# Attention beside a spectral filter: block 0 of x worked on alone at first, its key weights loaded behind it, the last chunk normalised in halves, and the planner's weights

## The chip, the cores and the metric

The kernel runs on one core of a Trainium2 chip, as one program. The metric is the device time in microseconds of one execution. Times from several executions are given as a median; the profile is taken from one execution.

## What is computed

The reference, cut to what matters (x has 2048 rows of 448 numbers in bfloat16, 16 heads of 28):

```
g   = sigmoid(sum(x * gate_w, -1))
q, k, v = split(x @ wqkv)                      # 16 heads of 28
p   = softmax(q @ k.T / sqrt(28))              # 2048 x 2048 for each head
a   = (p @ v) @ wo
b   = irfft2(rfft2(x) * (w_r + i w_i))         # over rows and columns
out = g * a + (1 - g) * b
```

## The kernel before

**Packs, units, chunks.** The heads are worked on in four groups of four, and the queries in four blocks of 512, which gives 16 chunks (group, query block). A chunk meets 16 key tiles of 128 keys, each a pack of four units, one for each head of the group: scores of 128 keys by 512 queries. There are 256 packs, 1024 units. A pack is taken either by ACT or by DVE. For ACT, a "tile" of two units is written by PE into one of two double banks (psA and psB, called "row" work), and one ACTIVATE takes the exponential of both units into the ring P of 20 units, or, for the first five packs, into slots of VS (line 902). For DVE, PE writes one unit at a time into a bank psX (`d_run`), DVE turns the scores into bits of an approximate power of two (line 931), and three shifted copies follow (line 937). In both cases PE then multiplies the probabilities by the values and sums into psV ("column" work, `pv_run`): one pass for a pack of ACT, four for a pack of DVE.

**The rest is background.** Transposes of x, projections to keys, queries and values, the four steps of the Fourier filter (f1, f2 and f3, i1, i2) and the output products are "units" of the planner: one or more PE operations into a psX bank and the evacuations that follow.

**The planner sets the order.** `Plan` runs while the program is built. It keeps a time for each engine and fills in the next operation by score: the due time of a unit, its `rush`, weights from `CFG`, and `seg`, which overrides these weights in each sixteenth of the stream (segment 17 holds once no score is left to be made). Only the order on each engine comes out of it; on the chip every engine runs its own list in that order and waits by semaphores. `pe_step` (line 640) chooses for PE: a ready tile for ACT goes first, and otherwise the offer with the lowest score that fits before the next tile is due. Offers come from value passes, open units, new units, scores for DVE (weight `w_d`) and "zero" matmuls. These multiply by zeros into an open accumulation or a free bank. `load` (line 259) sums the columns that PE worked in the last 3.413 us; under `z_hard` a zero matmul gets the score -20 ahead of everything, and under `z_soft` it is offered where there is nothing else. `step` (line 312) chooses for the other engines; ACT takes an exponential when one is ready, unless an operation of negative priority is, and it takes an operation that belongs to DVE (`alt`) only before the keys are complete (`early`).

**The head.** `loads` (line 1110) issues the constants and then the weights of the first group (keys, then queries; 112 columns each) on ACT's queue, and the four blocks of x on SP's, followed by the value weights and the rest. `head` (line 1186) makes for each block b of 512 rows two units "xT" of eight transposes, which wait only for that block's DMA; each is evacuated by DVE or ACT. `first` (line 1229) projects the keys of group 0 for block b and the queries of block 0: four matmul passes, a square on ACT, a norm product of PE with `selk` or `selrow` into the same bank ("sel"), and an evacuation to KT or QT with scale. Between them, DVE copies the key weights into the padded form Wk and POOL the query weights into Wq (line 1152). When the minimum over all keys is known, "w" computes a weight for each key (`o_wt`, line 1225), by which the values are multiplied (`weigh`, line 1346). Until then no value pass and no pack of DVE can start.

**The tail.** A chunk is normalised by way of DMAs (`norms`), except the last: `norm_last` (line 1522) takes 128 queries at a time, four times, on DVE. It transposes psV into osb, takes the reciprocal of the sums, multiplies by the gate, multiplies the values, and transposes the product into ON[3]. `final` (line 1535) makes for each of the 16 output tiles of 128 rows four products ("pre") and then the product with the last group; for the last four tiles the latter waits for `norm_last`. DVE evacuates tiles 0 to 11, and ACT tiles 12 to 15; a DMA writes them.

## Time and profile before

| | |
|---|---|
| time, median of 3 runs | 403.59 us (402.97 to 403.9) |
| time of the profiled execution | 402.86 us |
| its span | 401.1 us |
| PE busy | 385.3 us (96%) |
| DVE busy | 345.8 us (86%) |
| ACT busy | 384.2 us (96%) |
| POOL busy | 127.2 us (32%) |
| granted TensorE clock, mean | 0.999 |

The span runs from the first instruction's start to the last end that the profile holds; the time of the execution also has what lies around it. A group of the profile is named by its line, its engine, its operation and out<-in; behind "x" stands the number of instructions, and behind the bar the busy time and the mean of one in ns. Many helpers share a line (953 is every matmul), so tiles tell groups apart. A row of the order of time begins with its start and its length in us; the square bracket holds the idle time before it and what ended it. A row of the busy time by stage holds the stage, its length, the busy time of PE, weight loads, DVE, ACT and POOL with their counts, the granted clock, the share of the DMA engines and GB/s.

### The profile page before, as it was taken

What the parts mean: (1) busy time and instruction counts of PE and PEld (TensorE: products, weight loads), DVE (VectorE), ACT (ScalarE), POOL (GpSimd) and SP (SyncE); (2) the same over time, 40 slices, a digit from 0 to 9 for tenths busy, and PEclk for the clock granted to TensorE, in tenths of its full rate; (3) what the DMA queues carried; (4) which work ended last, traced back from release to release, by engine and by line L of the source; (5) the groups of instructions that cost most, each with busy time, mean ns of one, the idle gap of its engine ahead of it and who ended that gap; (6) DMA issues with size and microseconds to landing.
All of it is one profiled execution on the core that took longest, in us unless ns stands there. A gap on an engine that the chain in (4) does not pass through costs nothing.

```text
span 401.1 us, 12723 instructions
## 1 busy us (share of the span) xinstructions
PE 385.3 (96%) x5246; PEld 133.7 (33%) x5246; DVE 345.8 (86%) x633; ACT 384.2 (96%) x423; POOL 127.2 (32%) x176
## 2 busy tenths in 40 slices
PE   7999999999999999999999999999999999999995
PEld 3534433233333322332233222333334322223333
DVE  3649999978888898987899878899998999899994
ACT  3799999999999999999999999999999999999992
POOL 0121504532232136344334644547047520001000
PEclk9999999999999999999999999999999999999999
DMA  8700012100201202120112112022010001010012
GB/s 250 177 30 6 4 17 42 29 29 3 69 4 41 65 3 66 38 64 11 37 55 83 43 35 58 12 69 80 2 29 2 30 1 31 25 46 31 25 52 70
DMA packets 24394, 17.69 MB, mean 44 GB/s; under 512 B 15731, under 2 KB 19744, under 8 KB 24336
## 3 DMA queue, kind: packets, MB, share of 16 engines
q1 hardware_dynamic: 23264, 16.59, 15.2%
q8 instruction: 41, 0.67, 0.7%
q10 hardware_dynamic: 1072, 0.29, 0.4%
q14 instruction: 17, 0.14, 0.1%
HBM read 14.71 MB, written 1.97 MB: 42 GB/s over the span
## 4 chain that ended last, share of the span: by engine, by line
ACT 57%; PE 26%; issue 10%; DVE 4%; DMA 1%; ACTq 0%; DVEq 0%
ACT P L902 55%; PE psX L953 9%; PE psV L953 7%; PE psB L953 5%; PE psA L953 4%; DVE VS L931 2%; DMA Qf<-in_A_wqkv_dram 1%; ACT VS L902 1%; DVE VS L937 1%; PE psX L1198 1%; ACT xT L1205 0%; DVE Vb L1330 0%; ACT sq L1552 0%; DVE ost L1552 0%; DVE QT L1244 0%
## 5 line engine op out<-in xcount | busy, mean ns | idle before, releaser
L902 ACT ACTIVATE P<-psB 128x1024 bf16<-128x1024 f32 x198 | 215.5, 1088 | 0.2
L902 ACT ACTIVATE P<-psA 128x1024 bf16<-128x1024 f32 x198 | 215.5, 1089 | 0.1
L931 DVE TENSOR_SCALAR VS<-psX 128x512 int16<-128x512 f32 x212 | 139.4, 682 | 20.2 <-PE psX L953 19.6
L937 DVE TENSOR_SCALAR VS<-VS 128x2048 int16<-128x2048 int16 x159 | 103.5, 699 | 0.5
L953 PEld LDWEIGHTS <-KT 32*128 32x128 bf16 (+1 forms) x1040 | 46.6, 91 | 145.7 <-issue 142.4
L953 PE MATMUL psB<-QT,KT 32*128 32x512 bf16 x406 | 79.2, 382 | 5.4 <-ACT P L902 4.7
L953 PE MATMUL psA<-QT,KT 32*128 32x512 bf16 x406 | 79.7, 383 | 1.7 <-ACT P L902 1.3
L953 PE MATMUL psV<-VS,Vb 128*32 128x512 bf16 x868 | 76.3, 385 | 0.4 <-DVE osb L1510 0.2
L953 PE MATMUL psV<-P,Vb 128*32 128x512 bf16 x792 | 73.6, 385 | 0.0
L953 PE MATMUL psX<-QT,KT 32*128 32x512 bf16 x212 | 71.0, 383 | 0.5 <-DVE VS L931 0.2
L953 PEld LDWEIGHTS <-Vb 128*32 128x32 bf16 x1660 | 33.5, 94 | 57.5 <-issue 53.6
L1439 POOL TENSOR_TENSOR t<-FX,Wf 128x452 bf16<-128x452 f32 x32 | 31.7, 1013 | 41.5 <-DVE FX L1436 20.5
L1519 POOL TENSOR_TENSOR xtok<-osb,RB 128x512 bf16<-128x512 f32 x12 | 15.3, 1275 | 73.9 <-DVE VS L937 48.3
L1183 POOL TENSOR_TENSOR sq<-QT 128x512 bf16<-128x512 bf16 x16 | 16.6, 1041 | 41.2 <-DVE QT L1264 18.1
L1493 POOL TENSOR_TENSOR UZ<-tab 128x225 bf16<-128x225 f32 (+1 forms) x32 | 17.8, 583 | 23.1 <-DVE VS L937 19.1
L1183 POOL TENSOR_TENSOR sq<-KT 128x512 bf16<-128x512 bf16 x12 | 12.5, 1042 | 31.6 <-DMA omg<-gd 13.9
L953 PE MATMUL psX<-xT,Wk 112*32 112x512 bf16 x256 | 20.1, 383 | 0.0
L953 PE MATMUL psX<-Wv,xT 112*32 112x113 bf16 (+1 forms) x512 | 19.5, 262 | 0.0
L953 PE MATMUL psX<-xT,Wq 112*32 112x512 bf16 x240 | 19.5, 384 | 0.0
L1447 POOL TENSOR_TENSOR t<-t,t 128x226 bf16<-128x226 bf16 x32 | 17.5, 570 | 5.2 <-DVE VS L937 4.5
L953 PE MATMUL psX<-Bd,UZ 112*32 112x452 bf16 x256 | 18.7, 358 | 0.0
L953 PEld LDWEIGHTS <-xT 112*32 112x32 bf16 (+1 forms) x576 | 11.0, 96 | 10.5 <-issue 8.2
(104 smaller groups left out, 305.1 us busy)
## 6 DMA issues: line engine op xcount, KB each, us to landing
tab<-c_tab SPq DMA_DIRECT2D x16, 256.0 KB
RB<-rgd SPq DMA_DIRECT2D x60, 64.0 KB
xtok<-in_A_x_dram SPq DMA_DIRECT2D x4, 448.0 KB
out_dram<-ost SPq DMA_DIRECT2D x6, 224.0 KB
rs<-osb SPq DMA_DIRECT2D x60, 2.0 KB
Wf<-in_B_w_r_dram SPq DMA_DIRECT2D x31, 28.1 KB
Wf<-in_B_w_i_dram SPq DMA_DIRECT2D x31, 28.1 KB
Qf<-in_A_wqkv_dram SPq DMA_DIRECT2D x2, 294.0 KB
```

The costliest lines, as they stand in the source:

```text
L902: k.nc.scalar.activation(out=out, in_=k.psS[e["grp"]][:, 0:n, :], func=ACT.Exp, scale=LN2_128)
L931: k.nc.vector.tensor_scalar(out=k.VS[:, slot, 512 * h:512 * h + 512], in0=bank, scalar1=float(BITS0), scalar2=BITS_MIN, op0=ALU.add, op1=A ...
L937: k.nc.vector.tensor_scalar(out=k.VS[:, dst, :], in0=k.VS[:, src, :], scalar1=float(SHIFTS[v - 1]), scalar2=None, op0=ALU.add)
L953: self.nc.tensor.matmul(out, lhsT=lhsT, rhs=rhs, start=start, stop=stop, skip_group_check=True, **kw)
L1183: (self.nc.vector if e == "DVE" else self.nc.gpsimd).tensor_tensor(out=sq[:, :], in0=src, in1=src, op=ALU.mult)
L1198: nc.tensor.transpose(out=bb[0:C, 512 * ci + 128 * k:512 * ci + 128 * k + 128], in_=self.xtok3[:, 4 * b + k, C * c:C * c + C], identity=se ...
L1439: ts.append(pl.op("POOL", 1.07, lambda e, i=i, q=q: nc.gpsimd.tensor_tensor(out=self.t12[i][q][:, :].rearrange("p (r f) -> p r f", r=2), i ...
L1447: (nc.vector if e == "DVE" else nc.gpsimd).tensor_tensor(out=t1[:, FP * q:FP * q + FP], in0=t1[:, FP * q:FP * q + FP], in1=t2[:, FP - FP * ...
L1493: nc.gpsimd.tensor_tensor(out=z, in0=a, in1=b, op=ALU.subtract if q else ALU.add)
L1519: prev = pl.op("POOL", 1.3, lambda e, G=G, j=j: nc.gpsimd.tensor_tensor(out=self.ON[G][:, 512 * j:512 * j + 512], in0=self.osb[:, :], in1= ...
```

## The change

**Loads.** SP issues block 0 of x, then the key weights of group 0, then blocks 1 to 3. ACT's queue keeps the constants and the query weights. The planner's landing times for these DMAs are lower.

**Head.** Block 0's transposes, its keys and its queries get the highest rush (8) and the earliest places. The queries of block 0 are made right behind its keys, ahead of block 1. The transposes of block 1's second half wait for the norm product of block 0's keys, and those of blocks 2 and 3 for that of block 0's queries. ACT may evacuate transposes only of blocks 0 and 1 (`x_act=4`).

**Choice of PE.** While the load is under `z_hard`, every column operation with an efficiency over 0.8 gets the bonus of 20, not the zero matmul alone; the zero matmul's score is 9 before the bonus.

**Choice of ACT.** ACT also takes evacuations that belong to DVE once no score and no exponential is left.

**Tail.** `norm_last` takes 256 queries at a time, twice. Tiles 0 to 11 of the output may be evacuated by ACT.

**Weights.** `z_hard` is 3450 by default (was 3250), and many weights of segments are different.

The diff, cut:

```diff
@@ step
-            if eng == "ACT" and o.alt is not None and not early and o.eng != "ACT":
+            if eng == "ACT" and o.alt is not None and not early and o.eng != "ACT" and (any(self.s_left) or self.next_exp < len(self.tiles)):
                 continue
@@ pe_step
+        w = self.load(t) if any(self.s_left) and t >= self.zero_from else 1e9
+        hard = w < c["z_hard"] and self.started
+
-        def offer(score, kind, n, go):
+        def offer(score, kind, n, go, eff=1.0):
             nonlocal best
             cost = self.pe_cost(kind, n)
+            if hard and kind != "row" and eff > 0.8:
+                score -= 20.0
...
-        if any(self.s_left) and t >= self.zero_from:
-            w = self.load(t)
-            if w < c["z_hard"] or (best is None and w < c["z_soft"]):
-                hard = w < c["z_hard"] and self.started
-                if self.v_open(t) and self.started:
-                    offer(-20.0 if hard else 9.0, "col", 512, lambda: self.zero(t, "col", None))
...
+        if w < c["z_hard"] or (best is None and w < c["z_soft"]):
+            if self.v_open(t) and not self.started:
+                offer(9.0, "full", 512, lambda: self.zero(t, "full", None))
+            elif self.v_open(t) or fb:
+                offer(9.0, "col", 512, lambda: self.zero(t, "col", None if self.v_open(t) else fb[0]))
@@ CFG
+    last=((0, 2), (2, 2)), x_act=4,
-    z_hard=3250
+    z_hard=3450
     seg={
-        0: dict(d_open=4, w_hungry=0, z_hard=3550),
-        1: dict(d_open=4, z_hard=3550),
-        2: dict(w_new=2.0, z_hard=3550),
-        3: dict(pv_min=3, hungry=2),
-        4: dict(hungry=4),
-        5: dict(v2_due=3.1, hungry=4),
-        6: dict(hungry=4, prio_shift=3),
-        7: dict(w_pv=0.6, z_hard=3450, tol=0, v2_at=0.5, prio_shift=3),
+        0: dict(d_open=4, w_hungry=0, z_hard=3550, w_open=1.2),
+        1: dict(tol=0),
+        3: dict(tol=0.15),
+        4: dict(ahead=2, tol=0.15),
+        5: dict(v2_due=3.1, hungry=4, w_pv=0.6, tol=0.15),
+        6: dict(hungry=4, prio_shift=3, tol=0.15),
+        7: dict(w_pv=0.6, tol=0, v2_at=0.5, prio_shift=3),
...
-        10: dict(z_hard=3550),
-        11: dict(z_hard=3550),
+        10: dict(z_hard=3550, d_open=4),
+        11: dict(z_hard=3550, g_at=[1.1, 4.3, 8.0]),
...
-        13: dict(ring_urg=8, w_pv=0.2, prio_shift=3.5, z_hard=3550, d_urg=1, w_new=2.0),
-        14: dict(w_open=0.2, prio_shift=3.5, ahead=1, w_late=2, w_pv=0.2, ring_urg=6, w_new=2.0),
-        15: dict(prio_shift=3.5, w_open=0.2, w_late=2, w_pv=0.2, z_hard=3350, w_d=1.7, w_new=2.0),
-        16: dict(w_d=1.7, w_new=2.0, ring_urg=6),
-        17: dict(w_new=2.0),
+        13: dict(ring_urg=4, w_pv=0.2, prio_shift=3, z_hard=3550, d_urg=1, w_new=2.0, z_soft=3800, w_late=2),
+        14: dict(w_open=0.2, prio_shift=3.5, ahead=1, w_late=2, w_pv=0.2, ring_urg=4, w_new=2.0, w_due=4, pv_min=2, z_soft=3800),
+        15: dict(prio_shift=3.5, w_open=0.2, w_late=1, w_pv=0.2, z_hard=3350, w_new=1.2, w_due=4, pv_min=2, z_soft=3800),
+        16: dict(sw_pen=1.5),
+        17: dict(z_soft=3800, w_new=1.2),
@@ loads
-        self.d_w0 = [self.dma(..., 4.0, eng="ACT", prio=0) for i, o in ((0, D), (1, 0))]
         for b in range(4):
-            self.d_x.append(self.dma(..., (4.4, 5.6, 6.9, 8.2)[b], **fast))
+            self.d_x.append(self.dma(..., (4.0, 4.8, 5.55, 6.3)[b], prio=0 if b == 0 else 5, **fast))
+            if b == 0:
+                self.d_w0 = [self.dma(..., 4.2, eng=e, prio=1, ...) for i, o, e in ((0, D, "SP"), (1, 0, "ACT"))]
@@ head
-                u = pl.unit(-0.2, "xT", due=-1, rush=6.0 if b == 0 else CFG["x_rush"])
+                u = pl.unit(-0.2 if b == 0 else -0.185 + 0.01 * b, "xT", due=-1, rush=8.0 if b == 0 else CFG["x_rush"])
...
-                u.mm(tr, n=128, count=8, eff=0.0, deps=[self.d_x[b], self.d_cst])
+                u.mm(tr, n=128, count=8, eff=0.0, deps=[self.d_x[b], self.d_cst, sel[0] if (b, cp) == (1, 1) else sel[1] if b > 1 else None])
...
-                self.o_xT[b].append(u.use("DVE", dict(DVE=0.62, ACT=0.95), ev, alt="ACT", prio=2))
+                self.o_xT[b].append(u.use("DVE", dict(DVE=0.62, ACT=0.95), ev, alt="ACT" if 2 * b + cp < CFG["x_act"] else None, prio=2))
+            k = self.k_ready[0][b] = self.first(0, b, "k0", self.selk, 0)
...
+            if b == 0:
                 self.q_ready[0] = self.first(1, 0, "q0", self.selrow, 2)
...
+                sel = [self.sq_use[0], self.sq_use[2]]
@@ first
-        u = self.proj((-0.19 if b == 0 else -0.18) + 0.001 * b, which, 0, b, name, due=-1, rush=6.0 if b == 0 else CFG["k_rush"])
+        u = self.proj(-0.195 + 0.002 * which if b == 0 else -0.18 + 0.01 * b, which, 0, b, name, due=-1, rush=8.0 if b == 0 else CFG["k_rush"])
@@ norms, norm_last
-                self.o_last = [self.norm_last(t, prev) for t in range(4)]
+                self.o_last = sum((self.norm_last(t, n, prev) for t, n in CFG["last"]), [])
...
-        s = slice(128 * t, 128 * t + 128)
+        s = slice(128 * t, 128 * (t + n))
@@ final
-            evs.append(u.use(eng, dict(DVE=0.54, ACT=0.5), ev, deps=...))
+            evs.append(u.use(eng, dict(DVE=0.54, ACT=0.5), ev, alt="ACT" if j < 3 else None, deps=...))
```

51 lines of the change are left out of this document (24 added, 27 removed).

## The prediction

> **What bounds the kernel now.** I read the page first (busy shares, the chain that ended last), then the groups of instructions by line, then the busy time by stage, and last the order of time at the two ends.
>
> ```profile
> span 401.1 us, 12723 instructions
> ACT 57%; PE 26%; issue 10%; DVE 4%; DMA 1%; ACTq 0%; DVEq 0%
> L902 ACT ACTIVATE P<-psA 128x1024 bf16<-128x1024 f32 x198 | 215.5, 1089 | 0.1
> L902 ACT ACTIVATE P<-psB 128x1024 bf16<-128x1024 f32 x198 | 215.5, 1088 | 0.2
> L902 ACT ACTIVATE VS<-psB 128x1024 bf16<-128x1024 f32 x5 | 5.4, 1078 | 0.0
> L902 ACT ACTIVATE VS<-psA 128x1024 bf16<-128x1024 f32 x5 | 5.3, 1069 | 0.0
> L931 DVE TENSOR_SCALAR VS<-psX 128x512 int16<-128x512 f32 x212 | 139.4, 682 | 20.2 <-PE psX L953 19.6
> ```
>
> 198 + 198 + 5 + 5 = 406 exponentials of two units each go over ACT; the 212 of L931 are 53 packs of four units that DVE takes instead (812 + 212 = 1024 units). The chain is ACT for the most part, then PE. The groups add up to more than the span because an ACTIVATE's record overlaps the next one, so the step is read from start to start:
>
> ```profile
> 16.93 1.02 ACT L902 ACTIVATE VS<-psA 128x1024 bf16<-128x1024 f32 x1
> 17.85 1.02 ACT L902 ACTIVATE VS<-psB 128x1024 bf16<-128x1024 f32 x1
> 18.75 0.60 ACT L1235 ACTIVATE sq<-psX 128x512 bf16<-128x512 f32 x1
> 19.23 1.04 ACT L902 ACTIVATE VS<-psA 128x1024 bf16<-128x1024 f32 x1
> 20.13 1.06 ACT L902 ACTIVATE VS<-psB 128x1024 bf16<-128x1024 f32 x1
> 25.56 1.13 ACT L902 ACTIVATE VS<-psB 128x1024 bf16<-128x1024 f32 x1
> 390.35 1.02 ACT L902 ACTIVATE P<-psB 128x1024 bf16<-128x1024 f32 x1
> ```
>
> Undisturbed, six steps take 25.56 - 20.13 = 5.43 us, 0.905 each. From the first start to the last there are 405 steps in 373.42 us, 0.922 each: 405 x 0.905 = 366.5, so 6.9 us are lost in small gaps. The time is therefore: 16.93 us until the first exponential, 374.4 us of stream, some 9.7 us of tail, and 402.86 - 401.1 = 1.76 us around the span.
>
> **The head.** The chain at the start, and what stands beside it:
>
> ```profile
> 1.13 5.86 DMA Qf<-in_A_wqkv_dram
> 7.02 0.49 DVE Wk L1152 x4
> 7.51 0.60 DVE xT L1205
> 8.15 1.05 PE psX L1198 x16
> 9.21 0.98 PE psX L953 x16
> ...
> 4.74 1.10 PE L1198 MATMUL psX<-cst,xtok 128*112 128x128 bf16 x16
> 5.88 1.01 ACT L1205 COPY xT<-psX 112x1024 bf16<-112x1024 bf16 x1 [2.19 <-PE psX L1198]
> 0.74 1.84 SPq L1105 DMA_DIRECT2D xtok<-in_A_x_dram  x4
> 16.56 0.75 DVE L1244 TENSOR_SCALAR KT<-psX,onef 128x512 bf16<-128x512 f32 x1
> 9.75 0.95 POOL L1152 COPY Wq<-Qf 112x112 bf16<-112x112 bf16 x4 [9.31 <-DMA Qf<-in_A_wqkv_dram]
> 13.23 1.05 PE L953 MATMUL psB<-xT,Wq 112*32 112x512 bf16 x16 [0.65 <-ACT xT L1205]
> 4.70:9.20 4.50, 2.76 (x40) 2.23 (x43) 1.08 (x5) 1.42 (x2) 0.00 (x0) 1.00 1.10 332
> ```
>
> Block 0 of x is there at 4.74, but DVE stands at the weight copy until the key weights land at 6.99, and the first half's evacuation queues behind it to 8.11. Then block 1's transposes (8.15 to 9.20) go ahead of the key projection, and the query projection waits behind blocks 1 to 3 until 13.23. From 4.70 to 9.20 PE is busy 2.76 of 4.50 us. So the head has slack that an order can use.
>
> The change puts the key weights' DMA right behind block 0 in SP's queue and leaves the query weights second in ACT's, the place the keys had. Neither price is in the trace: the key weights land between 4.74 (with block 0) and 6.99 (as now); I take about 5.9, the middle. The query weights land by 6.99, since their place had that landing, and the POOL copy of 0.95 makes them usable at 7.97. The two halves of block 0 are evacuated by ACT until 6.89 and by DVE (0.60) before that, with the weight copy (0.49) on either side. The key projection starts at 6.93 at best, 8.15 at worst (DVE still at the copy first, as now). It takes about 1.05, so the queries start at 8.0 to 9.2. From the query projection's start to the first exponential the trace has 16.93 - 13.23 = 3.70, so the first exponential comes at 11.7 to 12.9. I take 12.1, nearer the early end because ACT's row at 5.88 does not move: **4.8 us earlier** (4.0 to 5.2).
>
> [...]
>
> What is late next? SP's later issues move back by one issue (four take 1.84, so 0.46 each), and blocks 1 to 3 arrive that much later plus the weights' bytes; PE's idle time hides it. The transposes of block 1's second half now wait for block 0's key norm matmul, those of blocks 2 and 3 for the query's. Behind them on PE stand only their own projections. Block 2's follow the first key projection now (9.21 + 0.98 = 10.2) and could go at about 10.3. Eight exponentials (7.2 us) use block 0 alone, so the keys of block 1 are needed at 19.3; now they are ready at 17.3 (16.56 + 0.75). But three things give some of it back.
>
> First, key squares on ACT. One of the three for blocks 1 to 3 lies inside the stream now and costs 19.23 - 17.85 - 0.905 = 0.475. All three will: **+0.95**.
>
> Second, the ring. The first five packs and 20 ring units cover 20 exponentials; the next needs a probability pass of PE to have freed its slot.
>
> ```profile
> 22.48 0.15 DVE L1215 TENSOR_REDUCE kminb<-kmin 128x1 bf16<-128x4 f32 x1
> 25.23 0.61 PE L953 MATMUL psV<-cst 128*32 128x512 bf16 x8
> 28.27 0.59 ACT L1225 ACTIVATE Vb<-psX 128x64 bf16<-128x64 f32 x1
> L953 PE MATMUL psV<-P,Vb x792: 377/389/391, 34.1 to 391.6; 128*32 128x512 bf16 x198
> L931 DVE TENSOR_SCALAR VS<-psX x212: 626/682/693, 30.2 to 385.5; 128x512 int16<-128x512 f32 x106
> ```
>
> Exponential 21 would be due at 12.1 + 20 x 0.905 + 3 x 0.475 = 31.6, while the first pass over P is at 34.1. If nothing behind the keys moves, ACT stalls 2.9 us (34.1 + 0.4 - 31.6). If the keys' end moves as much as the first exponential, it stalls 0. There is room: the minimum is known at 22.6 and its exponential comes at 28.27, with zero matmuls like those at 25.23 between. I take **+1.0**.
>
> Third, DVE's share. Its packs start only behind the keys, at 30.2, and 53 fit until 386.2: one in 6.72 us, 0.595 units per us, beside ACT's 2 / 0.922 = 2.17. An advance of 4.8 - 0.95 - 1.0 = 2.85 us on ACT is 6.2 units, and 6.2 / 2.76 = **2.2 us** at the end of the stream.
>
> **The order inside the stream** is retuned: thresholds for zero matmuls, weights by segment, and the new rule that in the "hard" state useful column work, no longer zeros alone, gets the bonus of 20. The same 406 exponentials are to be fed, and 45 to 360 shows an ACT that is full:
>
> ```profile
> 45.00:360.00 315.00, 307.74 (x4067) 100.49 (x4065) 282.71 (x497) 314.85 (x344) 114.56 (x141) 1.00 0.13 35
> ```
>
> The 6.9 us of gaps bound it below (all gone) and above (twice as many); PE at 307.74 of 315 speaks against much gain. I take 0, the value of this row, and keep about -2 and +2 for the range.
>
> **The tail.**
>
> ```profile
> 392.00:396.40 4.40, 3.71 (x80) 1.99 (x73) 4.27 (x22) 1.06 (x2) 0.00 (x0) 1.00 0.04 10
> L1529 DVE STREAM_TRANSPOSE osb<-psV 128x128 f32<-128x128 f32 x4 | 1.1, 303 | 1.7 <-PE psV L953 1.7
> 394.77 0.97 PE psB L953 x20
> 395.82 0.54 ACT sq L1552
> 396.40 0.37 PE psB L953 x4
> 396.78 0.97 PE psX L953 x20
> ```
>
> DVE is busy 4.27 of 4.40 us: four chains of five short instructions, and two output evacuations between them that ACT may now take (it has 1.06 of 4.40). An instruction over 256 columns costs between 0.30 (as for 128) and 0.60 (twice); I take 0.43, near the fixed part, so two chains are some 3.1 us for 4.6 and end about 395.2. But PE is next: it works from the stream's end without a hole except from 395.74 to 396.40, where a last product waits for ACT. Only these **0.7 us** go. Ends: -1.6 when one output tile (0.97) also moves into the stream, +0.4 when the first half, ready later than the first quarter, keeps PE waiting.
>
> **Sum**, against the profiled execution of 402.86: -2.2 - 0.0 - 0.7 = -2.9, **400.0 us**. The median of the runs shown, 403.59, is 0.73 higher; on it the sum would be 400.7. The range holds both.
>
> **Rivals.**
>
> *Larger gain.* Keys land with block 0 (0.4 more) and no ring stall (1.0 more): the advance is 4.25, worth 3.3 at the end; with 1.2 us of the gaps gone and the same tail, 402.86 - 5.2 = 397.6. For it: the slack from 22.6 to 28.27, and DVE busy 1.08 of 4.50 us at the start. Against it: PE's fill in the stream. Chance 0.23.
>
> *The ring takes it.* The keys of blocks 1 to 3 end no earlier or, behind exponentials, 1 us later: the stall is 2.9 to 3.9, the advance 0 to 0.95, the time 401.4 to 402.2 with the tail and about 403 without. This is also the case in which the weights come no earlier and block 0 alone gains little. Chance 0.09.
>
> *Slower: DVE loses packs.* The new bonus goes to column work, not to the row scores that feed DVE, and the threshold rises from 3250 to 3450 in several segments. DVE waits 19.6 us for these scores already (the L931 row). Each pack lost means four units, two exponentials, 1.81 us on ACT. With 2.9 gained elsewhere it decides from the second lost pack on; at 50 packs the time is 400.0 + 5.4 = 405.4. Against it: scores that run together with an ACT tile do not pass through this choice. Chance 0.11.
>
> *Slower: the clock.*
>
> ```profile
> 396.40:401.10 4.70, 1.32 (x24) 0.59 (x23) 0.00 (x0) 1.06 (x2) 0.00 (x0) 0.88 0.43 140
> ```
>
> The granted clock is 1.00 in every stage above and falls to 0.88 in the last one, where PE is busy 1.32 of 4.70. Fewer zero matmuls could let it fall inside the stream: a stage of 20 us, nearly all PE, would take 2.4 us longer at 0.88. From 25 us of such stages on the gain is gone; at two stages, 404.8. [...] Chance 0.05.
>
> **How the numbers follow.** Forecast (398.5 to 402): 0.52; larger gain (396 to 398.5): 0.23; ring 0.09; lost packs 0.11; clock 0.05. Faster by over 0.2% (0.8 us, about what a measurement of this kernel can tell from no change): 0.52 + 0.23 + 0.04 = 0.79; within it, most of the ring's case, 0.05; slower 0.16. The range 396.3 to 403.5 leaves out the slower cases and the farthest part of the larger gain.
>
> **What would show it.** First exponential at 11.7 to 12.9; key weight copy on DVE before 7; first query projection before 9.3. Exponential 21 in step or late: the ring. The count of L931: 212 or 208 here, 204 and less for lost packs. Steps of ACT still 0.92 on the mean. In the tail, fewer and longer DVE transposes, two of each, output evacuations on ACT, and no PE hole behind the first final products. Wrong if the first exponential stays behind 14, if the clock row drops below 1.00 before 390, or if the tail from the last exponential on is longer than 10.7 us.

## The result and the profile after

The changed kernel takes 400.35 us (median of 4 runs, 399.91 to 400.7), the kernel before 403.5 (4 runs beside it). The ratio is 0.9922, interval 0.9905 to 0.9939: faster by some 3 us. The forecast was 400.0. The profiled execution is 400.49 with a span of 398.7, against 402.86 and 401.1: the two that the profiles show are 2.4 apart, the medians 3.15, and the account below is one of the 2.4.

The page of the changed kernel: its span, the chain by engine, and the two groups in which the share of work between ACT and DVE is read (count, busy time and mean ns, idle time ahead).

```profile
span 398.7 us, 12653 instructions
PE 46%; ACT 44%; issue 8%; DMA 1%; DVE 1%; ACTq 0%; DVEq 0%
L901 ACT ACTIVATE P<-psB 128x1024 bf16<-128x1024 f32 x198 | 219.9, 1110 | 0.0
L930 DVE TENSOR_SCALAR VS<-psX 128x512 int16<-128x512 f32 x212 | 138.9, 681 | 17.3 <-PE psX L952 16.4
```

The counts are those of before: 212 units for DVE, so 53 packs, and 406 exponentials. No pack was lost or won. The chain now has PE at 46% beside ACT at 44%, where ACT had 57% and PE 26%. Hardly any idle time is booked ahead of the exponentials (0.0 in this row; the one long stall, shown below, is booked to a small instruction that ran in it), and the chain now passes back and forth between the two engines.

The order of time at the start of the changed kernel:

```profile
4.82 1.95 PE L1202 MATMUL psX<-cst,xtok 128*112 128x128 bf16 x16
5.27 0.49 DVE L1153 COPY Wk<-Qf 112x112 bf16<-112x112 bf16 x4 [0.76 <-DMA Qf<-in_A_wqkv_dram]
5.61 0.95 POOL L1153 COPY Wq<-Qf 112x112 bf16<-112x112 bf16 x4 [5.17 <-DMA Qf<-in_A_wqkv_dram]
6.81 0.69 DVE L1209 COPY xT<-psX 112x1024 bf16<-112x1024 bf16 x1 [1.05 <-PE psX L1202]
7.78 1.05 PE L952 MATMUL psX<-xT,Wk 112*32 112x512 bf16 x16
8.65 1.04 PE L952 MATMUL psX<-xT,Wq 112*32 112x512 bf16 x16
...
12.65 1.02 ACT L901 ACTIVATE VS<-psA 128x1024 bf16<-128x1024 f32 x1 [1.10 <-PE psB L952]
```

The key weights are copied from 5.27 on and the query weights from 5.61 on, where before DVE and POOL had to wait until 7.02 and 9.75. The query projection starts at 8.65 instead of 13.23. The first exponential starts at 12.65 instead of 16.93: 4.28 us are won here.

The 16 transposes of block 0 take 1.95 us here and took 1.10 before. PE was at half pace until 6.76: the transposes start every 0.107 us, before every 0.056, and zero matmuls of 448 columns start every 0.374 us ahead of that time and 0.190 apart behind it. The trace's record of the granted clock begins only at 6.76 too (before at 4.05); where there is no record, the tables print 1.00. Before, the zero matmuls too start every 0.374 us up to 4.09 and 0.190 apart behind that, and the transposes follow at 4.74. The group of the transposes on psX (56 of them) has a mean of 249 ns here, and of 223 in the two kernels below that have the old tail and the last write on ACT's queue, with the head as it is here. So the slow transposes belong to the execution and not to the order. In the kernel of "The same with weights fitted anew" below (mean 223 ns) those of block 0 take 1.10:

```profile
4.87 1.10 PE L1203 MATMUL psX<-cst,xtok 128*112 128x128 bf16 x16 [0.18 <-DMA xtok<-in_A_x_dram]
```

Its query projection starts at 8.07 and its first exponential at 12.07, 0.58 sooner than here and by the same 4.00 us apart.

How much of that arrives at the end is read from ACT's exponentials in order. The same view of the changed kernel, the end of the keys and the first value passes:

```profile
27.43 0.58 PE L952 MATMUL psX<-Wv,xT 112*32 112x113 bf16 x32
...
31.33 0.65 ACT L1227 ACTIVATE Vb<-psX 128x64 bf16<-128x64 f32 x1
31.44 1.40 ACT L901 ACTIVATE P<-psB 128x1024 bf16<-128x1024 f32 x1
34.23 1.25 PE L952 MATMUL psV<-P,Vb 128*32 128x512 bf16 x20
34.35 0.21 ACT L1358 ACTIVATE ge<-glog 128x16 f32<-128x16 f32 x1 [1.51 <-DVE glog L1334]
34.71 1.02 ACT L901 ACTIVATE P<-psA 128x1024 bf16<-128x1024 f32 x1
...
388.22 1.04 ACT L901 ACTIVATE P<-psB 128x1024 bf16<-128x1024 f32 x1
```

The step from 31.44 to 34.71 is 3.27 where 0.905 is undisturbed. This is exponential 21, which needs a slot of the ring, and the pass that frees it starts at 34.23, where it started at 34.1 before. (ACT's next instruction in that step is a small one for the gates, which waited for DVE and would alone have held ACT until 34.56. The exponential itself comes 0.48 us behind the pass; in a run below without such an instruction in its stall it is 0.48 as well, so it is the ring that ends last, if only by 0.15.) Before, exponential 21 started at 35.79 and waited for nothing:

```profile
35.79 1.25 ACT L902 ACTIVATE P<-psA 128x1024 bf16<-128x1024 f32 x1
```

So of 4.28 us 1.08 are left at this point, and at the last exponential (390.35 before, 388.22 now) 2.13. The account of the span is then: first exponential -4.28; from the first start to the last 388.22 - 12.65 = 375.57 instead of 373.42, +2.15; from the last start to the end 398.7 - 388.22 = 10.48 instead of 10.75, -0.27. The sum is -2.4, the difference of the two spans.

Why the pass over P came no earlier is read from PE between the first exponential and that pass, in the busy time by stage (columns: stretch, length, PE, weight loads, DVE, ACT, POOL, granted clock, DMA share, GB/s), first before, then in the changed kernel:

```profile
16.93:34.05 17.12, 16.97 (x359) 7.61 (x359) 10.84 (x22) 17.12 (x21) 4.16 (x4) 1.00 0.14 41
12.65:34.23 21.58, 21.17 (x467) 10.41 (x468) 12.71 (x25) 20.18 (x24) 4.12 (x4) 1.00 0.29 73
```

PE is full in both. The order of PE leaves 24 of block transposes and 32 more matmuls of the key projection behind the first exponential, where before all transposes were done ahead of it, and 64 more matmuls of the value projection stand in the stretch. The 20 zero matmuls that it held before are gone. So the work taken out of the head came back between the first exponential and the first slot that is freed.

The end of the changed kernel, in order of time:

```profile
389.94 0.78 DVE L1533 STREAM_TRANSPOSE osb<-psV 128x256 f32<-128x256 f32 x2 [0.99 <-PE psV L952]
...
394.38 0.36 PE L952 MATMUL psX<-Bd,xT 128*32 128x448 bf16 x4
394.85 0.53 ACT L1556 CAST sq<-psX 128x448 bf16<-128x448 f32 x1 [0.41 <-PE psX L952]
395.92 0.40 SPq L1104 DMA_DIRECT2D out_dram<-sq  x1
```

DVE now has two transposes over 256 columns each way instead of four over 128. PE's last product ends at 394.38 + 0.36 = 394.74, 6.52 us behind the last exponential's start (388.22). Before, the last products ended at 396.78 + 0.97 = 397.75, 7.40 us behind it (390.35): 0.88 less, and no wait of PE stands in these rows. But the last write is issued at 395.92, although ACT has finished the tile at 394.85 + 0.53 = 395.38. SP is busy with its issues until then:

```profile
L1104 SPq DMA_DIRECT2D out_dram<-sq x4: 332/394/1608, 393.3 to 395.9; - x4
```

This is the row of SP's four last writes by line (least, median and largest ns). One issue of the four took 1.608 us (from 393.75 to 395.36), and the last write stood behind it for 0.54 us. What was on the way beside it is in the DMA queues of the stretch from 393.7 to 395.4:

```profile
q8 instruction: 1, 0.02, 4.6%
```

This is one packet of 16 KB of instructions, on the way from 393.73 to 394.98; the issue ends 0.38 us behind it, about the median of the four issues (0.394). Before, such a packet ended at 396.66, and the issue that it met, 0.67 us long from 396.38, ended 0.38 behind it too; the median of the four there is 0.375. That the loading of code holds SP, and not the writes on the way, is the author's reading of these times; no run was made without such a packet.

Two more stretches of the changed kernel, in the same columns:

```profile
4.70:9.20 4.50, 4.38 (x55) 3.32 (x59) 1.18 (x5) 2.33 (x3) 0.95 (x4) 1.00 1.06 355
28.80:35.00 6.20, 5.96 (x179) 3.42 (x171) 4.35 (x11) 4.54 (x8) 0.00 (x0) 1.00 0.02 8
```

PE is busy 4.38 of 4.50 us in the stretch from 4.70 to 9.20, in which it had 2.76 (0.85 of this is the slow transposes). From 6.76 to the end of the span the granted clock does not fall, though the zero matmuls behind the head went from 44 to 20 (8 on psV and 12 on psX).

### The profile page after: what moved, and what is told of

It is laid out like the page before. It is cut to its first block, busy times and chain, and to the rows that moved or that the text cites. A ratio compares the mean times of both kernels' runs of the same rounds, so it can differ in the third digit from the quotient of the medians.

```text
span 398.7 us, 12653 instructions
## 1 busy us (share of the span) xinstructions
PE 386.0 (97%) x5221; PEld 134.9 (34%) x5221; DVE 344.3 (86%) x622; ACT 383.6 (96%) x424; POOL 126.9 (32%) x176
## 4 chain that ended last, share of the span: by engine, by line
PE 46%; ACT 44%; issue 8%; DMA 1%; DVE 1%; ACTq 0%; DVEq 0%
ACT P L901 44%; PE psX L952 16%; PE psV L952 13%; PE psB L952 8%; PE psA L952 8%; DMA xtok<-in_A_x_dram 1%; PE psX L1202 1%; ACT VS L901 0%; DVE KT L1246 0%; DVE QT L1246 0%; ACT Vb L1227 0%; DVE Vb L1348 0%; PE psV L1202 0%; ACT sq L1556 0%; ACT sq L1237 0%
## 5 line engine op out<-in xcount | busy, mean ns | idle before, releaser
L901 ACT ACTIVATE P<-psB 128x1024 bf16<-128x1024 f32 x198 | 219.9, 1110 | 0.0
L901 ACT ACTIVATE P<-psA 128x1024 bf16<-128x1024 f32 x198 | 219.6, 1109 | 0.1
L936 DVE TENSOR_SCALAR VS<-VS 128x2048 int16<-128x2048 int16 x159 | 101.5, 689 | 0.4
L952 PEld LDWEIGHTS <-KT 32*128 32x128 bf16 (+1 forms) x1040 | 47.8, 91 | 145.3 <-issue 141.0
L1184 POOL TENSOR_TENSOR sq<-KT 128x512 bf16<-128x512 bf16 x12 | 12.5, 1040 | 22.6 <-DVE KT L1174 17.1
L952 PE MATMUL psX<-Bd,UZ 112*32 112x452 bf16 x256 | 19.6, 358 | 0.0
```

The source lines that it names most:

```text
L901: k.nc.scalar.activation(out=out, in_=k.psS[e["grp"]][:, 0:n, :], func=ACT.Exp, scale=LN2_128)
L936: k.nc.vector.tensor_scalar(out=k.VS[:, dst, :], in0=k.VS[:, src, :], scalar1=float(SHIFTS[v - 1]), scalar2=None, op0=ALU.add)
L952: self.nc.tensor.matmul(out, lhsT=lhsT, rhs=rhs, start=start, stop=stop, skip_group_check=True, **kw)
L1184: (self.nc.vector if e == "DVE" else self.nc.gpsimd).tensor_tensor(out=sq[:, :], in0=src, in1=src, op=ALU.mult)
```

## The experiments

Theory: the head's earlier start makes the gain, the square stalls and the ring give part of it back, the tail adds a little, and the rule and weights inside the stream only have to keep the order from losing it. Rivals: the gain is due to the rule and the weights alone; a part works without the others; the stall behind the keys is due to late weights of the keys, so that taking these earlier would win more.

### The parts by themselves

**The head alone**: the kernel before with the new loads, the new `head` and `x_act`, and the old zero rule and weights. Zero matmuls that are chosen early read other zero columns, since the constants are there later:

```diff
+        rhs = k.ost[:, 0, :] if soon else k.cst[:, 0:512]
...
-        self.d_w0 = [self.dma(..., eng="ACT", prio=0) for i, o in ((0, D), (1, 0))]
+        self.d_w0 = []
...
+            if b == 0:
+                self.d_w0 = [self.dma(..., eng=e, prio=1, ...) for i, o, e in ((0, D, "SP"), (1, 0, "ACT"))]
```

> The kernel before with the head of the change alone (loads, order of blocks, x_act), the old rules and weights of the stream and the old tail. Its early zero matmuls stream 448 columns of zeros in place of 512 of the constants. Theory (the order of the head moves the first exponential, and the late end of the keys gives about half of it back): first exponential at 12.4 to 13.0, a stall of ACT near exponential 20, time 1.0 to 2.5 us below before. Rival (the gain of the change is the retuned stream; the ring takes all that the head gives): first exponential at 12.4 to 13.0 too, but the time within 0.5 us of before.

Measured: 416.22, ratio 1.0319 (1.0303 to 1.0334), 13 us slower, beyond what either theory allowed. The first exponential does start at 12.52. But the fortieth starts at 54.15, where it started at 53.68 before: the head's gain is used up by then. The rest comes late in the stream. Exponential 320 starts at 312.90, and then, in the order of time of this kernel:

```profile
315.95 4.79 POOL L1497 TENSOR_TENSOR UZ<-tab 128x225 bf16<-128x225 f32 x6 [0.61 <-DVE tab L1491]
...
317.64 4.25 DVE L938 TENSOR_SCALAR VS<-VS 128x2048 int16<-128x2048 int16 x5
321.81 0.68 DVE L1514 COPY osb<-psV 128x512 f32<-128x512 f32 x1
323.70 2.39 PE L954 MATMUL psV<-P,Vb 128*32 128x512 bf16 x20
324.47 1.02 ACT L902 ACTIVATE P<-psA 128x1024 bf16<-128x1024 f32 x1 [10.33 <-PE psV L954]
```

It is the end of a chunk (the step between the exponentials is 11.57 us). POOL's products of the filter come one behind the other, DVE's shifted copies of the chunk's last pack stand between and behind them, so this pack's value passes come late, psV is evacuated only at 321.81, the next chunk's passes start at 323.70, and ACT stands with a full ring for 10.33 us. The list was made for another head, and here it is bad. This run tells that the head does not carry its gain by itself, but not what the head is worth, since the weights are fitted to another order.

**The tail alone**: `norm_last` over 256 columns twice, `alt="ACT"` in `final`, and the new choice of ACT in `step`, in the kernel before.

```diff
-                self.o_last = [self.norm_last(t, prev) for t in range(4)]
+                self.o_last = sum((self.norm_last(t, n, prev) for t, n in CFG["last"]), [])
...
+            evs.append(u.use(eng, dict(DVE=0.54, ACT=0.5), ev, alt="ACT" if j < 3 else None, ...))
```

> The kernel before with the tail of the change alone (halves, output evacuations also on ACT), head and stream as before. Theory (PE is next in the tail, so only the hole before the last products goes, and the last write takes some of it): from the start of the last exponential to the end 10.75 becomes 10.1 to 10.6, time 0.1 to 0.7 us below before. Rival (the normalisation on DVE is what the end waits for): 1.2 us or more below before.

Measured: 402.37, ratio 0.9985 (0.9977 to 0.9994), 0.6 us faster; from the last exponential's start (390.06) to the end of the span (400.3) it takes 10.24 us, in the range expected.

**The stream alone**: the new rule, thresholds and weights, old head and tail.

```diff
+            if hard and kind != "row" and eff > 0.8:
+                score -= 20.0
...
-    z_hard=3250
+    z_hard=3450
...
-        0: dict(d_open=4, w_hungry=0, z_hard=3550),
+        0: dict(d_open=4, w_hungry=0, z_hard=3550, w_open=1.2),
```

> The kernel before with the retuned stream alone (bonus rule, thresholds, weights by segment), old head and old tail. Theory: first exponential at 16.9, gaps in the stream 5 to 7 us for 6.9, time 0 to 1.2 us below before. Rival (the retuned stream is where the gain comes from): 2.5 us or more below before. A third (DVE loses packs): fewer than 212 conversions of scores and a slower time.

Measured: 409.99, ratio 1.0172 (1.0156 to 1.0189). Not the cause of the gain, but a miss in size: no theory had 7 us more. It is again one stall at a chunk's end, a step of 9.31 us (310.15 to 319.46); the exponential that ends it, in this kernel's order of time:

```profile
319.46 1.02 ACT L901 ACTIVATE P<-psA 128x1024 bf16<-128x1024 f32 x1 [8.13 <-PE psV L952]
```

Both runs left open whether the parts or only the ill-fitting weights were measured. So the two were run again with `seg` weights fitted to each:

**Head and tail with the old rule, refitted.** The two edits of the head and the tail together, and:

```diff
-    seg={ the weights of before }
+    seg={ weights fitted to this head under the old rule }
```

> The kernel before with the head and the tail of the change, the old rule for zero matmuls, and weights by segment fitted anew until the order has no stall beyond the first 40 exponentials. Early zero matmuls stream 448 columns of zeros in place of 512 of the constants. Theory (the head's gain needs the new rule: under the old one ACT stalls 3.4 us near 19 and 4.1 us near 32, as in the head alone, and the 40th exponential comes at 54, not 52): no stall near 312 any more, first exponential at 12.5, time 401.5 to 403.5, no better than the tail alone. Rival (the loss of the head alone was the misfit only): 400.5 or less.

Measured: 403.03, ratio 0.9994 (0.9984 to 1.0005): no gain, though the first exponential starts at 12.35 and nothing stalls near 312. Its order of time shows where the 4.6 us went:

```profile
18.69 1.10 ACT L902 ACTIVATE VS<-psB 128x1024 bf16<-128x1024 f32 x1
19.59 1.18 ACT L1239 ACTIVATE sq<-psX 128x512 bf16<-128x512 f32 x2
22.11 1.02 ACT L902 ACTIVATE VS<-psA 128x1024 bf16<-128x1024 f32 x1 [0.23 <-PE psB L954]
29.35 0.54 ACT L1229 ACTIVATE Vb<-psX 128x64 bf16<-128x64 f32 x1
34.94 0.98 PE L954 MATMUL psX<-Wv,xT 112*32 112x113 bf16 x64
35.96 0.82 PE L954 MATMUL psV<-P,Vb 128*32 128x512 bf16 x12
36.44 1.02 ACT L902 ACTIVATE P<-psA 128x1024 bf16<-128x1024 f32 x1 [2.96 <-PE psV L954]
```

Two stalls take it: the step at 18.69 is 3.42 us with the squares, and the one at 32.33 is 4.11. The keys' weights come at 29.35, 2 us earlier than in the changed kernel, and yet the first pass over P comes at 35.96, 6.6 us behind them, for the value projections still stand ahead of it. In the changed kernel most of these lie before the weights, and the pass follows them by 2.9 us (31.33 to 34.23). From the first exponential to the first pass over P this kernel has:

```profile
12.35:35.96 23.61, 23.29 (x476) 11.72 (x476) 12.52 (x24) 20.39 (x24) 4.16 (x4) 1.00 0.22 62
```

PE is as full as in the changed kernel, but 56 of these matmuls are zeros, where the changed kernel has none in its 21.58 us. The pass comes 2.03 us later behind the first exponential, most of the 2.7 us between the two medians. Useful work in the place of zeros is what the rule asks for; the weights by segment differ too, and no run changes the rule alone in an order that is otherwise the same.

**The old head with the new rule, refitted.** The edit of the stream, and:

```diff
-    seg={ the weights of the change }
+    seg={ weights fitted to the old head under the new rule }
```

> The kernel before with the new rule and thresholds, old head and old tail, and weights by segment fitted anew until the order has no stall of ACT near 310. Theory (the rule alone saves zero matmuls, not time of ACT): first exponential at 16.6, time within 1 us of before. Rival (the rule is where the gain comes from): 401 or less.

Measured: 404.11, ratio 1.0026 (1.0013 to 1.0039), first exponential at 16.96, no stall at 310, one DVE pack fewer (208 units). The lost pack is 1.81 us, so without it this order would be at some 402.3 (an estimate, 404.11 - 1.81). Neither order has the gain. How much of it each half would have in its best order is not shown by these two runs: one pack, or a worse fit, is as large as what is compared here, as the nudged cost below shows.

### Undone or doubled in the changed kernel

**The key weights' DMA back on ACT's queue**, with every engine's compute order as it was:

```diff
+                self.d_w0[0].emit = lambda e=None: self.nc.scalar.dma_start(out=self.raw[0:C, 0, :, 0:112], in_=w3[:, :, D:D + 112])
```

> The changed kernel with every instruction in the order it has, except that the DMA of the first key weights is issued on ACT's queue ahead of the query weights, as in the kernel before. Theory (the place in SP's queue right behind block 0 brings the key weights from 7.0 to 5.3): the copy on DVE starts at 6.5 to 7.2, the query copy on POOL at 7 or later, the first exponential comes 0.8 to 2 us later than 12.65, and the time is 0.3 to 1.2 us longer, as the ring's stall takes part of it. Rival (the DMA's place is nothing, the order of blocks is all): first exponential within 0.3 us and time within 0.3 us of the changed kernel.

Measured: 403.01, ratio 0.9989 (0.9978 to 1.0001), so 2.7 us above the changed kernel's median, and more than expected. Its order of time:

```profile
7.64 0.49 DVE L1154 COPY Wk<-Qf 112x112 bf16<-112x112 bf16 x4 [2.60 <-DMA Qf<-in_A_wqkv_dram]
10.07 0.94 POOL L1154 COPY Wq<-Qf 112x112 bf16<-112x112 bf16 x4 [9.63 <-DMA Qf<-in_A_wqkv_dram]
10.40 1.07 PE L952 MATMUL psX<-xT,Wq 112*32 112x512 bf16 x16 [1.01 <-POOL Wq L1154]
14.41 1.02 ACT L901 ACTIVATE VS<-psA 128x1024 bf16<-128x1024 f32 x1 [1.09 <-PE psB L952]
390.52 1.04 ACT L901 ACTIVATE P<-psB 128x1024 bf16<-128x1024 f32 x1
```

The key weights are at DVE 2.4 us later (7.64 against 5.27) and the query weights, now second on ACT's queue, 4.5 later (10.07 against 5.61). The key projection loses only 0.29 by it (8.07 for 7.78), the query projection 1.75 (10.40 for 8.65), and it waits for the query weights. So what counts here is less that the key weights come early than that they no longer stand ahead of the query weights. The first exponential moves by 1.76, and the last by 2.30 (388.22 to 390.52). Nothing of the delay is won back: the order is fixed, and the ring stall of 3.27 us comes again, 1.76 later. In this fixed list the place of one DMA in a queue is worth nearly the whole gain; with a list fitted to it, it might be worth less. Of the two weight loads, the one that is second on ACT's queue is copied from 9.75 on before and from 10.07 on here, and from 5.61 on where it is the only one there.

**The old tail** in the changed kernel:

```diff
-                self.o_last = sum((self.norm_last(t, n, prev) for t, n in CFG["last"]), [])
+                self.o_last = [self.norm_last(t, prev) for t in range(4)]
...
-            evs.append(u.use(eng, dict(DVE=0.54, ACT=0.5), ev, alt="ACT" if j < 3 else None, ...))
+            evs.append(u.use(eng, dict(DVE=0.54, ACT=0.5), ev, ...))
```

> The changed kernel with the old tail (quarters, output evacuations of tiles 0 to 11 on DVE alone). Theory (the tail gives 0.3 to 0.7, of which the last writes take some): 0.2 to 0.9 us above the changed kernel. Rival (with the new stream the tail is PE alone): within 0.2 us.

Measured: 401.26, ratio 0.995 (0.9935 to 0.9965), 0.9 above the changed kernel's median, as expected. In the profiles the tail is 399.1 - 388.32 = 10.78 us for 10.48, so 0.3 of the 0.9 is seen in it; where the rest lies is not shown. The hole of PE that the prediction quoted is back, in the order of time of this kernel:

```profile
394.39 0.37 PE L952 MATMUL psB<-Bd,xT 128*32 128x448 bf16 x4 [0.69 <-ACT sq L1554]
```

**A planner cost nudged**, nothing else:

```diff
-    dve_op1=0.605
+    dve_op1=0.61
```

> The changed kernel with one cost of the planner nudged, DVE's conversion of scores from 0.605 to 0.61, which the chip does not see but by the order that comes out. Theory (the weights by segment are fitted to one order; parts taken alone lost 7 to 13 us because the fit was gone, not because the part is bad): 2 us or more above the changed kernel, with fewer packs of DVE (under 212 conversions) or a stall of ACT behind 60 us. Rival (the order is robust, and the losses of the parts alone show the parts): within 1 us of the changed kernel.

Measured: 403.79, ratio 1.001 (0.9994 to 1.0025). The head is the same (first exponential at 12.70), but the groups on this kernel's page count two packs fewer for DVE and four exponentials more for ACT:

```profile
L901 ACT ACTIVATE P<-psB 128x1024 bf16<-128x1024 f32 x200 | 223.0, 1115 | 0.0
L930 DVE TENSOR_SCALAR VS<-psX 128x512 int16<-128x512 f32 x204 | 133.8, 681 | 20.3 <-PE psX L952 19.9
```

Four exponentials at 0.905 are 3.6 us, and the span is 3.2 longer. A cost changed by 5 ns in the planner takes the whole gain, by lost packs, at the price (1.81 us for each) that the prediction gave in a rival.

**The last write on ACT's queue.**

```diff
-                self.dma(..., 2.0, [evs[t]], prio=0)
+                self.dma(..., 2.0, [evs[t]], eng="ACT" if t == 15 else "SP", prio=0)
```

> The changed kernel with the last of the four writes of the last chunk issued on ACT's queue and not on SP's. Theory (SP's issue of the second of these writes took 1.6 us and pushed the last to 395.9, half a us behind its evacuation): the last write is issued within 0.1 us of its evacuation's end, time 0.3 to 0.6 us below the changed kernel. Rival (the writes' bytes on the way set the end): within 0.2 us.

Measured: 400.05 (4 runs, 399.93 to 400.14), ratio 0.991 (0.9896 to 0.9925). In its order of time the write no longer waits for SP:

```profile
394.81 0.53 ACT L1556 CAST sq<-psX 128x448 bf16<-128x448 f32 x1 [0.41 <-PE psX L952]
395.37 0.36 ACTq L1104 DMA_DIRECT2D out_dram<-sq  x1
```

It is issued 0.03 us behind its evacuation (395.34). The tail is 398.1 - 388.18 = 9.92 us instead of 10.48. But in this execution SP's own third write, whose issue took 0.78 us, was out at 395.20, ahead of that evacuation, so the last write would hardly have waited on SP either. The median is only 0.3 lower than the changed kernel's and the intervals overlap, so neither the profile nor the times settle what the other queue is worth. This is the lowest median of all versions run.

**The same with weights fitted anew:**

```diff
-    seg={ the weights of the change }
+    seg={ weights fitted to the changed kernel once more }
```

> The changed kernel with the last write on ACT's queue and the weights by segment fitted a little further, head, rule and tail as they are. Theory: 0.3 to 0.8 us below the changed kernel, nearly all of it from the write. Rival (the further fit follows the planner's costs and not the chip): no better than the last write alone.

Measured: 400.4, ratio 0.9929 (0.9917 to 0.9941); first exponential 12.07, last 387.68, 212 units on DVE. Its last write too is issued 0.03 us behind its evacuation, and its tail is 398.4 - 387.68 = 10.72. A further fit to the planner's costs wins nothing on the chip.

### Is the stall due to late key weights?

In the changed kernel the products for the weight of each key (`wk`) have `eff=0.0` and so no bonus, and the value projections go ahead of them. **With `eff=0.9`** they get it:

```diff
-            u.mm(lambda bank, i=i: wk(bank, i), n=130, count=4, eff=0.0, deps=[m])
+            u.mm(lambda bank, i=i: wk(bank, i), n=130, count=4, eff=0.9, deps=[m])
```

> The changed kernel with one number different: the four PE operations that make the weights of the keys count with an efficiency of 0.9 for 0.0, so that they get the bonus of the hard state too and no longer stand behind the value projections. Theory (ACT stalls 2.4 us at exponential 21 because the keys' weights come at 31.3, as their PE work is pushed behind): the exponential for the weights comes at 27 to 29, no step over 1.2 us beside those with squares, time 1.2 to 2.4 us below the changed kernel. Rival (the stall comes from the values, which are made at the same time): the weights come earlier but the stall stays over 1.5 us, and the time is within 0.5 us of the changed kernel.

Measured: four executions at 410.05 to 414.86, with a ratio of 1.0216 (1.0179 to 1.0253), and two at 417.93 and 421.44; the profile is of the one at 417.93. The weights' exponential does come at 28.50 instead of 31.33. The stall is no longer one step of 3.27 but three of 1.68, 1.52 and 2.12, and something new shows in the busy time by stage of this kernel:

```profile
28.80:35.00 6.20, 6.20 (x78) 1.85 (x74) 3.21 (x6) 4.17 (x7) 0.00 (x0) 0.50 0.02 9
```

The granted clock is 0.50 in the stage where it was 1.00, and PE, all of the time busy, gets 78 matmuls through instead of 179. The same happened between 70 and 90 us (0.65 and 0.66 in its halves), two packs were lost (204 units), and a step of 7.25 us came at 319.7. In the execution of 410.05 the mean clock was 1.00: the 9.7 us that it lies above the changed kernel are about the two packs (3.6) and that step (7.25 - 0.905 = 6.3) of the profile, and the longer executions have a lower mean clock (down to 0.963). Too much changed at once. So the order was fitted again, with the bonus given without counting these products as load:

```diff
-            u.mm(lambda bank, i=i: wk(bank, i), n=130, count=4, eff=0.0, deps=[m])
+            u.mm(lambda bank, i=i: wk(bank, i), n=130, count=4, eff=0.0, deps=[m]).bonus = 1.0
```

> The changed kernel with the bonus of the hard state given to the four PE operations that make the weights of the keys, without counting them as load, and weights by segment fitted anew. Theory now (from 28 to 36 us PE is full, so an earlier weight moves the stall and does not remove it; and where these thin matmuls stand together the granted clock falls): the exponential for the weights at 28 to 29, matmul passes of 0.6 us there, time not under the changed kernel. Rival (the stall was the late weights): 1 us or more below the changed kernel.

Measured: 402.44 (401.03 to 406.58), ratio 0.999 (0.9968 to 1.0012). The weights' exponential comes at 28.18, and again the clock falls:

```profile
24.65:28.07 3.42, 3.02 (x102) 1.92 (x93) 1.87 (x5) 3.42 (x5) 1.84 (x2) 1.00 0.08 30
28.07:31.48 3.41, 3.41 (x76) 1.69 (x74) 1.92 (x4) 2.73 (x5) 0.00 (x0) 0.50 0.03 12
34.89:38.31 3.42, 3.42 (x130) 1.96 (x122) 2.68 (x7) 3.39 (x4) 0.00 (x0) 1.00 0.02 5
```

The fall begins at 28.07 and ends at 34.89. The order of time ahead of it shows the products with 4 columns standing close together:

```profile
26.22 0.35 PE L954 MATMUL psX<-cst,KT 128*128 128x4 bf16 x8
...
27.04 0.35 PE L954 MATMUL psX<-cst,KT 128*128 128x4 bf16 x8
```

In the changed kernel the two sets of 4-column products stand 3.7 us apart (26.61 and 30.30), with value projections between, and the clock keeps 1.00. The last section sums what PE did in such stretches: the two sets fall into one stretch of 3.41 us here, and into two there. That the products are what lets the clock fall is argued from these counts and orders, not shown by a run of its own.

The clock does not fall in every execution: in three of the twelve its mean was 1.000, and they took 401.03 to 401.16, in the others it was 0.983 to 0.996, and they took 401.85 to 406.58. So with the clock kept this order is still 0.7 above the changed kernel, but it also has one pack of DVE fewer (208 units, 1.81 us). What earlier weights of the keys are worth with the clock and all packs kept is open; 401.1 - 1.81 = 399.3 is an estimate of it.

## Why the prediction was right, and where not

The forecast of 400.0 lies 0.35 from the median, in part by luck: it was worked out for the profiled execution, which changed by 2.4 for the 2.9 forecast, and terms that were off by more offset each other.

**The head: right.** First exponential at 11.7 to 12.9, taken 12.1; measured 12.65, the gain 4.28 for 4.8. The parts: key weights at 5.27 (taken 5.9), key projection at 7.78 (6.93 to 8.15), query projection at 8.65 (8.0 to 9.2). From there it took 4.00 for the 3.70 that before had. The weights came even earlier than taken, but the second half of block 0 was evacuated from 6.81 on, behind its transposes, and so the early end was not reached. The 0.85 us by which these were slower is PE's half pace up to 6.76, which the prediction did not have; in the kernel whose transposes took 1.10 the first exponential came at 12.07. In the two kernels with the head as here and the mean of 223 ns it came at 12.62 and 12.54; there PE stood 0.9 and 0.7 us ahead of its transposes, mostly for x, and 0.1 here.

**Key squares: right.** Three steps of 1.38 to 1.39 in the changed kernel, for example 17.67 to 19.05 in its order of time, each 0.475 over; the prediction's +0.95 is exact.

**The ring: mis-sized.** Taken +1.0, measured 3.27 - 0.905 = 2.36. The prediction had the bound, 2.9 if nothing behind the keys moves, and at the first exponential measured it is 34.1 + 0.4 - (12.65 + 18.1 + 1.43) = 2.3. It took a third of it because there was room from 22.6 to 28.27. The step that failed is "the keys' end moves": the first pass over P stayed (34.1 and 34.23). The room was only that of the 20 zero matmuls, and the transposes and key projections that left the head filled it and more: PE is busy 21.17 of the 21.58 us between the first exponential and the pass. The end of the keys even moved back by 3 us (28.27 to 31.33), as the order has query and value projections ahead of key blocks 2 and 3 and of the keys' weights; under the old rule it moved back too, to 29.35. The runs with earlier weights (28.50, 28.18, and 29.35 with the old rule) show that the weights' time alone does not decide: the first pass followed them later, or the clock fell.

**DVE's share: wrong in form.** The prediction multiplied the advance on ACT by 2.17 / 2.76, as if DVE's rate were fixed. DVE started later (34.2 for 30.2 in the first start of its groups), ended at 386.3 for 385.5, and did the same 53 packs. The count is a whole number that the list fixes. When it moves, it moves in steps of 1.81 us: two packs with the nudged cost, one with the new rule on the old head.

**The order inside the stream: taken 0, measured -0.95.** Over the whole stream the excess above 405 x 0.905 grew from 6.9 to 9.05. Up to 40 us it grew by 3.1 (squares 0.95, ring 2.36, the rest less); behind 40 us it fell from 5.9 to 4.97. This lies in the range given (-2 to +2).

**The tail: right in mechanism, mis-sized.** Taken -0.7, measured -0.27. The transposes of psV over 256 columns took 0.428 us on the mean of their group (taken 0.43), the hole of PE went, and PE was done 0.88 sooner behind the last exponential; then SP's issue of 1.608 us took 0.54 back, which the prediction did not have. Alone it was -0.6 by the medians, undone +0.9 (of it 0.3 in the profiled tail).

So the sum came about by terms that offset: the ring was 1.4 too small, the head's gain 0.5 and the tail's 0.4 too large, and against them stood 0.95 in the stream, 0.2 elsewhere up to 40 us and the 0.6 that the factor for DVE had taken off. The sum in the prediction was -2.9 on the span, the measured one -2.4. **The rivals** did not happen here, but three were met close by: lost packs with the nudged cost, the clock in the two kernels with early weights of the keys, and weights no earlier with the DMA back on ACT's queue. (In the rival of the clock, 20 us at 0.88 cost 20 / 0.88 - 20 = 2.7 us and not 2.4.)

## What to carry to other kernels

An earlier start is worth what is left of it at the first resource that is handed back late; here it was a ring of 20 slots, and the gain fell from 4.28 to 1.08 us at exponential 21. Look for the first instruction that frees a slot, and ask whether the change moves that one, and what the engine that executes it has to do before it. Where the order is a fitted list, a part taken out or put in alone measures the misfit (13 and 7 us here) until the list is fitted again, and a gain of 3 us can hang on one whole pack or on one DMA's place in a queue.

## What the runs showed of the hardware

**The granted clock.** The rows show it at 1.00 and at 0.50, and the values between stand for stretches that hold both: the 0.88 from 396.40 to 401.10 before is 3.59 us at 1.00 and 1.11 at 0.50. Before, the full clock lasts from 4.05 to 399.99, which is 395.946 us or 116 times 3.4133, and the row from 400 to 401 has 0.50. In the changed kernel it lasts from 6.76 to beyond the end of the span, 392.533 us or 115 times 3.4133. The fall of the refitted kernel, from 28.07 to 34.89, is twice 3.41. So the traces of before and of the changed kernel were cut into windows of 3.413 us, and for each the matmul records were summed: columns, times the share of 128 rows and of 128 output columns that the matmul uses, so that a matmul marked 32*128 counts a quarter. In the refitted kernel the stretch ahead of the fall (24.65 to 28.07), which holds both sets of 4-column products, has 2723. The changed kernel has 4086 and 3739 in the two windows that hold its sets, and its clock stays. Before and in the changed kernel the last windows have 2473 and 0, with the half clock behind them; the lowest sums of the other 229 are 3564 and 3397, and behind these the clock stays. PE's busy time does not tell them apart: it is 3.02 of 3.41 us ahead of the fall, and 2.90 in the changed kernel from 317.38 to 320.79, where the clock stays. No run was made to test whether these sums decide. Sixteen products of 4 columns add 64 to the sum, and their rows show 0.70 us of PE.

**Issues of DMAs.** One write's issue on SP took 1.608 us where the median of the four is 0.394. It ended 0.38 us behind a packet of 16 KB of instructions. The same shows throughout the changed kernel's trace: SP has six more issues of over 0.74 us between 50 and 390 us, and each ends 0.30 to 0.38 behind the end of such a packet.
